# Top-k attention with a smooth-ReLU MLP: top-k over pairs of scores, and the mask by a rectifier and a subtraction

## The chip, the cores and the metric

The kernel runs on one core of a Trainium2 chip. A core has five engines with queues of their own: TensorE (PE; its weight loads are shown apart as PEld), VectorE (DVE), ScalarE (ACT), GpSimd (POOL) and SyncE (SP), which here issues the DMAs. Each engine works off its instructions in one fixed order, and semaphores make it wait for others. The metric is the device time of one execution in microseconds. The kernel before takes 2017.08 us (median of 3 runs, 2016.96 to 2017.25).

## The reference

Two blocks, one behind the other. In attention (8 batches, 8 heads, 576 rows, head size 64), each row keeps only its 32 largest scores:

```python
scores = scale * np.matmul(q, k.transpose(0, 1, 3, 2))
kth = np.partition(scores, -top_k, axis=-1)[..., -top_k:-top_k + 1]
mask = scores >= kth
scores = np.where(mask, scores, -1000000000.0)
scores = scores - np.max(scores, axis=-1, keepdims=True)
attn = np.exp(scores)
attn = attn / (np.sum(attn, axis=-1, keepdims=True) + 1e-09)
return np.matmul(attn, v).astype(np.float32)
```

Its output, 4608 rows of 512, goes through an MLP of width 2048: `h = x @ w_in`, then 0 where h <= -1, h where h >= 1, and (h + 1)² / 4 between, then `@ w_out`. The two weights come as float64, everything else as float32.

## The kernel before, in words

**Steps.** A batch's 576 rows are four tiles of 128 rows and a tail of 64. A step handles one pair of heads of one tile (for a tail, two pairs of heads in the 128 partitions); there are 144 steps, `m` counts them. Each step has five parts:

- `scores` (L194): PE multiplies queries by keys into PSUM banks (L206), ACT copies them with the scale to `s` in SBUF (L209), [128, 2, 576]: 128 rows, two heads, 576 scores.
- `top_k` (L211), all on DVE: MAX8 (L218) gives the eight largest of a row, MATCH_REPLACE8 (L221; the profile shows a short MATCH_VALUE_LOAD ahead of it) strikes them out. Four rounds of MAX8 and three of striking out, for each of two heads, give the 32 largest; the last of `tops` is the threshold.
- `weights` (L230): POOL makes the negated threshold `nkth` (L233) and `nb` (L235). For each head ACT applies the mask, a Prelu with a huge slope below the threshold (L228), then Exp with the row's sum (L239). DVE makes the reciprocal of the sum (`z` L241, `rz` L242), POOL scales the row by it (L244).
- `transpose_w` (L247): PE transposes the weights (L254, L257), ACT copies them from PSUM to `wT` and `wTt` (L255, L258).
- `values` (L261): PE multiplies by v into `po` (L269, L277), ACT copies the result to `xT` (L282, L284), the MLP's input.

**The MLP.** It runs over chunks of one or two row tiles. `hidden` (L297) makes 128 hidden units: PE into a bank `ph` (L300; three banks), ACT `r` (L304), POOL its square (L306), DVE the clamp `g` (L307). `final` (L310) multiplies by w_out into `py` (L315), ACT copies it to `y` (L319; two buffers), SP stores it.

**The weights.** `weight_piece` (L78) turns 512 float64 columns into float32, as SP loads them: DVE takes the bits apart (L85, L86, L90), ACT converts the low word (L92) and takes a magnitude (L97), POOL puts them together (L93, L94), DVE writes the result (L98). There are 32 such pieces. The tiles between have one buffer each, so a piece follows another.

**Order.** PE's order is the program's. Pass `m` of the main loop (L407) puts on it: `values` of step m-2, scores of m+1, MLP work, `transpose_w` of m-1, queries and keys to come, MLP work. `top_k` and `weights` of step m come in the same pass. `advance` (L365) hands out the MLP's work, by costs, evenly over the steps left, but only as far as the pieces are converted; `convert` (L357) converts `PER_STEP` (L53) pieces a step. The order on the other engines is made when the program is built, from the dependences and estimated costs. The tiles of scores, transposes and values share a ring of four PSUM banks (tag `a`): PE can't go on until ACT has emptied one.

**Loads.** SP issues all DMAs in one queue: values and keys of the next batch, queries two tiles ahead (tails in `q_tl`, L136, two buffers), weight pieces, and the stores of `y`.

Of the kernel before, what the change touches and what calls it, by code (L numbers as in the profile page):

```python
# [11 lines left out]
U32 = mybir.dt.uint32  # L12
AF = mybir.ActivationFunctionType
# [3 lines left out]
TOP_K = 32  # L17
# [4 lines left out]
def kernel(  # L22
# [30 lines left out]
    PER_STEP = 3  # L53

    const = ctx.enter_context(tc.tile_pool(name="const", bufs=1))
    xtp = ctx.enter_context(tc.tile_pool(name="xtp", bufs=3))
    stage = ctx.enter_context(tc.tile_pool(name="stage", bufs=2))
    att = ctx.enter_context(tc.tile_pool(name="att", bufs=2))
    ps = ctx.enter_context(tc.tile_pool(name="ps", bufs=1, space=PSUM))

# [15 lines left out]
    WC = 512  # L76
# [37 lines left out]
    def whole(x, b):  # L114

        return x[b, :, 0:SM, :].rearrange("h (p c) d -> p h c d", c=NT)

    def load_values(b):
        v_in = stage.tile([P, H, NT, D], F32, name="v_in")
        nc.sync.dma_start(out=v_in, in_=whole(v, b))  # L120
        v_tl = v_tails[b % 2]
        for j in range(2):
            nc.sync.dma_start(out=v_tl[0][j * TL:(j + 1) * TL, j::2, :],
                              in_=v[b, j::2, SM:S, :].rearrange("h p d -> p h d"))
        for hp in range(NHP):
            g = hp % 2
            nc.sync.dma_start(out=v_tl[1][g * TL:(g + 1) * TL, 2 * hp:2 * hp + 2, :],
                              in_=v[b, 2 * hp:2 * hp + 2, SM:S, :].rearrange("h p d -> p h d"))
        return v_in, v_tl

    def load_queries(b, t):
        if t < NT:
            q_in = stage.tile([P, H, D], F32, name="q_in", bufs=2)
            nc.sync.dma_start(out=q_in, in_=whole(q, b)[:, :, t, :])
        else:
            q_in = stage.tile([TL, H, D], F32, name="q_tl", bufs=2)  # L136
            nc.sync.dma_start(out=q_in, in_=q[b, :, SM:S, :].rearrange("h p d -> p h d"))
        return q_in


    def main(i):
        return slice(0, SM) if i == 0 else slice(TL, S)

    def tail(i):
        return slice(SM, S) if i == 0 else slice(0, TL)

    def pieces(i, j, c0, c1):

        if i == j:
            return [(c0, c1, c0)]  # L150
        cuts = [(0, TL, SM), (TL, S, 0)] if i else [(0, SM, TL), (SM, S, 0)]
        return [(max(a, c0), min(b, c1), o + max(a, c0) - a) for a, b, o in cuts if max(a, c0) < min(b, c1)]


    def keys_of(b):

        kT = stage.tile([P, NHP, S], F32, name="kT")
        v_in, v_tl = load_values(b)
        k_tl = stage.tile([TL, H, D], F32, name="k_tl", bufs=1)
        nc.sync.dma_start(out=k_tl, in_=k[b, :, SM:S, :].rearrange("h p d -> p h d"))  # L160
        for hp in range(NHP):
            k_in = stage.tile([P, NT, 2, D], F32, name="k_in")
            for j in range(2):
                nc.sync.dma_start(out=k_in[:, :, j, :], in_=whole(k, b)[:, 2 * hp + j])
            pt = ps.tile([P, NT, P], F32, name="pk", tag="a", bufs=4)
            for c in range(NT):
                nc.tensor.transpose(pt[:, c, :], k_in[:, c].rearrange("p j d -> p (j d)"), ident)
            for j in range(2):
                d = slice(j * D, (j + 1) * D)
                nc.scalar.copy(kT[d, hp, main(j)], pt[d].rearrange("p c n -> p (c n)"))  # L170
            if hp == 0:
                pt = ps.tile([P, NHP, TL], F32, name="pkt", tag="a", bufs=4)
                for h2 in range(NHP):
                    nc.tensor.transpose(pt[:, h2, :], k_tl[:, 2 * h2:2 * h2 + 2].rearrange("p j d -> p (j d)"),
                                        ident[0:TL, 0:TL])
                for j in range(2):
                    d = slice(j * D, (j + 1) * D)
                    nc.scalar.copy(kT[d, :, tail(j)], pt[d])
            yield dict(kT=kT, v=v_in, v_tl=v_tl)

    def queries_of(q_in, t):
        n = P if t < NT else TL
        qT = stage.tile([P, NHP, n], F32, name="qT" if t < NT else "qTt")
        pt = ps.tile([P, NHP, n], F32, name="pq", tag="a", bufs=4)
        for hp in range(NHP):
            nc.tensor.transpose(pt[:, hp, :], q_in[:, 2 * hp:2 * hp + 2].rearrange("p j d -> p (j d)"),
                                ident[0:n, 0:n])
        nc.scalar.copy(qT, pt)
        return qT
# [4 lines left out]
    def scores(st):  # L194
        t, hp, kT, qT = st["t"], st["hp"], st["keys"]["kT"], st["qT"]
        st["s"] = s = att.tile([P, 2, S], F32, name="s", bufs=3)
        for hf in range(2):
            sp = [ps.tile([P, SH], F32, name="sp", tag="a", bufs=4) for _ in range(2)]
            c0, c1 = hf * SH, (hf + 1) * SH
            for i in range(2):  # L200
                for j in ([i] if t < NT else [0, 1]):
                    d = slice(j * D, (j + 1) * D)
                    g = hp if t < NT else hp + i
                    o = sp[i] if t < NT else sp[i][j * TL:(j + 1) * TL]
                    for a0, a1, k0 in pieces(i, j, c0, c1):
                        nc.tensor.matmul(o[:, a0 - c0:a1 - c0], qT[d, g, :], kT[d, g, k0:k0 + a1 - a0],  # L206
                                         start=True, stop=True)
            for i in range(2):
                nc.scalar.activation(s[:, i, c0:c1], sp[i], AF.Copy, scale=SCALE)  # L209

    def top_k(st):  # L211
        s = st["s"]
        rest = att.tile([P, 2, S], F32, name="rest", bufs=1)
        st["tops"] = tops = att.tile([P, 2, TOP_K], F32, name="tops", bufs=3)
        src = s
        for r in range(0, TOP_K, 8):
            for i in range(2):
                nc.vector.max(out=tops[:, i, r:r + 8], in_=src[:, i, :])  # L218
            if r + 8 < TOP_K:
                for i in range(2):  # L220
                    nc.vector.match_replace(out=rest[:, i, :], in_to_replace=tops[:, i, r:r + 8],  # L221
                                            in_values=src[:, i, :], imm_value=LOWEST)
                src = rest
# [3 lines left out]
    def mask(x, nkth):  # L227
        nc.scalar.activation(x, x, AF.Prelu, bias=nkth, alpha=FAR)  # L228

    def weights(st):  # L230
        s, tops = st["s"], st["tops"]
        nkth = att.tile([P, 2], F32, name="nkth")
        nc.gpsimd.tensor_scalar(nkth, tops[:, :, TOP_K - 1], -1.0, 1.0, ALU.mult, ALU.mult)  # L233
# [151 lines left out]
    for got in keys_of(0):  # L385
        keys[0] = got
# [78 lines left out]
```

## Time and profile before

| | |
|---|---|
| median of 3 runs | 2017.08 us |
| the profiled execution | 2018.67 us |
| its span, first to last instruction | 2016.9 us |
| mean granted TensorE clock | 0.927 |
| first 33 us: loads, first keys | PE busy 11.6, DVE 10.9 us |
| MAX8 at 128x576 (1152 of them) | 748 to 750 ns each |
| MATCH_REPLACE8 at 128x576 (864) | 743 ns each |
| mask and Exp on ACT, 128x576 | 772 and 770 ns each |
| scaling on POOL, 128x576 | 768 ns each |
| two-input operation on POOL, 128x256 and 128x512 | 612 and 1271 ns each |

The profile gives for each engine the busy time, in slices and by groups of instructions with one line, and for each wait the instruction that ended it. A mean duration of one instruction is longer than the distance between the starts of two, since one begins before the other has ended. "PE sp L206 <- ACT xT L282: 54.3, 33, 5.1" means that the matmuls of line 206 waited 54.3 us in all, 33 times and 5.1 us at the longest, and that ACT's instruction of line 282 ended the wait. A granted clock of 1.0 is TensorE's full speed.

### The profile page before, as it was taken

What the parts mean: (1) busy time and instruction counts of PE and PEld (TensorE: products, weight loads), DVE (VectorE), ACT (ScalarE), POOL (GpSimd) and SP (SyncE); (2) the same over time, 40 slices, a digit from 0 to 9 for tenths busy, and PEclk for the clock granted to TensorE, in tenths of its full rate; (3) what the DMA queues carried; (4) which work ended last, traced back from release to release, by engine and by line L of the source; (5) the groups of instructions that cost most, each with busy time, mean ns of one, the idle gap of its engine ahead of it and who ended that gap; (6) DMA issues with size and microseconds to landing.
All of it is one profiled execution on the core that took longest, in us unless ns stands there. A gap on an engine that the chain in (4) does not pass through costs nothing.

```text
span 2016.9 us, 29329 instructions
## 1 busy us (share of the span) xinstructions
PE 1717.6 (85%) x10128; PEld 1175.6 (58%) x10128; DVE 1608.3 (80%) x3648; ACT 1075.0 (53%) x2589; POOL 537.6 (27%) x1003
## 2 busy tenths in 40 slices
PE   3245488989989999989898999888999999998999
PEld 2243266557566666656565666656474765765666
DVE  4878789989897887889786887888787787968861
ACT  4545546565555654565555555565454555545442
POOL 2564522213221221213121222213131231321321
PEclk7667798999999999989998999999999999999999
DMA  6232200100011001100011000110010000000000
GB/s 162 78 92 75 68 14 18 41 22 12 21 30 30 22 3 29 33 22 11 21 30 29 22 1 23 28 35 11 14 33 21 17 6 11 6 16 6 1 11 11
DMA packets 102803, 57.45 MB, mean 28 GB/s; under 512 B 85760, under 2 KB 93952, under 8 KB 102656
## 3 DMA queue, kind: packets, MB, share of 16 engines
q1 hardware_dynamic: 102656, 55.59, 10.0%
q8 instruction: 80, 1.31, 0.3%
q14 instruction: 67, 0.55, 0.1%
HBM read 46.14 MB, written 9.44 MB: 28 GB/s over the span
## 4 chain that ended last, share of the span: by engine, by line
DVE 53%; PE 19%; ACT 12%; POOL 10%; issue 6%; DMA 1%; SPq 0%; POOLq 0%; DVEq 0%; ACTq 0%
DVE tops L218 27%; DVE rest L221 20%; PE py L315 9%; PE ph L300 4%; ACT s L228 4%; ACT s L239 3%; DVE g L307 3%; POOL s L244 3%; ACT s L209 2%; POOL r L306 2%; PE sp L206 2%; POOL low L93 2%; PE po L269 2%; POOL low L94 2%; PE pw L254 2%
## 5 line engine op out<-in xcount | busy, mean ns | idle before, releaser
L300 PE MATMUL ph<-xT,w_in 128*128 128x256 f32 (+1 forms) x2816 | 560.4, 355 | 72.0 <-DVE g L307 71.8
L218 DVE MAX8 tops<-rest 128x8 f32<-128x576 f32 x864 | 619.5, 748 | 0.1
L315 PE MATMUL py<-w_out,g 128*128 128x512 f32 x1152 | 558.6, 630 | 45.1 <-DVE w_out L98 39.5
L300 PEld LDWEIGHTS ph<-xT,w_in 128*128 128x128 f32 x2816 | 466.2, 197 | 158.0 <-DVE g L307 87.9
L221 DVE MATCH_REPLACE8 rest<-tops,rest 128x576 f32<-128x576 f32 x576 | 424.1, 743 | 0.0
L315 PEld LDWEIGHTS py<-w_out,g 128*128 128x128 f32 x1152 | 217.5, 199 | 306.1 <-issue 238.0
L228 ACT ACTIVATE s<-s,nkth 128x576 f32<-128x576 f32 x288 | 214.4, 772 | 315.4 <-POOL nkth L233 315.2
L218 DVE MAX8 tops<-s 128x8 f32<-128x576 f32 x288 | 205.9, 750 | 202.7 <-ACT s L209 202.7
L244 POOL TENSOR_SCALAR s<-s,rz 128x576 f32<-128x576 f32 x288 | 217.6, 768 | 382.0 <-DVE rz L242 243.1
L306 POOL TENSOR_TENSOR r<-r 128x256 f32<-128x256 f32 (+1 forms) x352 | 187.8, 540 | 423.6 <-ACT r L304 418.4
L206 PE MATMUL sp<-kT,qT 64*128 64x288 f32 x1024 | 196.8, 452 | 60.2 <-ACT xT L282 51.2
L304 ACT ACTIVATE r<-ph,half 128x256 f32<-128x256 f32 (+1 forms) x352 | 148.2, 433 | 172.8 <-PE ph L300 141.3
L255 ACT COPY wT<-pw 128x512 f32<-128x512 f32 x288 | 155.9, 587 | 132.8 <-PE pw L254 131.7
L239 ACT ACTIVATE s<-s,nb 128x576 f32<-128x576 f32 x288 | 221.6, 770 | 1.2
L254 PE MATMUL pw<-ident,s 128*128 128x128 f32 x1152 | 163.5, 288 | 68.8 <-POOL s L244 64.1
L209 ACT ACTIVATE s<-sp 128x288 f32<-128x288 f32 x576 | 198.7, 410 | 36.3 <-PE sp L206 34.7
L221 DVE MATCH_REPLACE8 rest<-tops,s 128x576 f32<-128x576 f32 x288 | 212.6, 743 | 0.0
L254 PEld LDWEIGHTS pw<-ident,s 128*128 128x128 f32 x1152 | 142.9, 149 | 119.5 <-POOL s L244 72.6
L307 DVE SCALAR_TENSOR_TENSOR g<-ph,r 128x256 f32<-128x256 f32 (+1 forms) x352 | 128.6, 368 | 76.4 <-POOL r L306 71.3
L233 POOL TENSOR_SCALAR nkth<-tops 128x2 f32<-128x2 f32 x144 | 29.1, 202 | 571.1 <-DVE tops L218 571.1
L206 PEld LDWEIGHTS sp<-kT,qT 64*128 64x128 f32 x1024 | 108.4, 194 | 108.0 <-ACT xT L282 66.0
L269 PEld LDWEIGHTS po<-wT,v_in 128*64 128x64 f32 x2048 | 120.1, 143 | 85.6 <-issue 41.3
(51 smaller groups left out, 1086.7 us busy)
## 6 DMA issues: line engine op xcount, KB each, us to landing
q_in<-in_q_dram SPq DMA_DIRECT2D x32, 256.0 KB, 3.1
v_in<-in_v_dram SPq DMA_DIRECT2D x8, 1024.0 KB, 5.9
k_in<-in_k_dram SPq DMA_DIRECT2D x64, 128.0 KB, 3.2
raw<-in_moe_w_in_dram SPq DMA_DIRECT2D x16, 512.0 KB, 3.9
raw<-in_moe_w_out_dram SPq DMA_DIRECT2D x16, 512.0 KB, 3.5
out_dram<-y SPq DMA_DIRECT2D x32, 256.0 KB, 2.3
v_tail<-in_v_dram SPq DMA_DIRECT2D x16, 64.0 KB, 2.5
k_tl<-in_k_dram SPq DMA_DIRECT2D x8, 128.0 KB, 3.2
```

What stands on the lines that cost most here:

```text
L206: nc.tensor.matmul(o[:, a0 - c0:a1 - c0], qT[d, g, :], kT[d, g, k0:k0 + a1 - a0], start=True, stop=True)
L209: nc.scalar.activation(s[:, i, c0:c1], sp[i], AF.Copy, scale=SCALE)
L218: nc.vector.max(out=tops[:, i, r:r + 8], in_=src[:, i, :])
L221: nc.vector.match_replace(out=rest[:, i, :], in_to_replace=tops[:, i, r:r + 8], in_values=src[:, i, :], imm_value=LOWEST)
L228: nc.scalar.activation(x, x, AF.Prelu, bias=nkth, alpha=FAR)
L239: nc.scalar.activation(s[:, i, :], s[:, i, :], AF.Exp, bias=nb[:, i:i + 1], accum_out=z[:, i:i + 1])
L244: nc.gpsimd.tensor_scalar(s[:, i, :], s[:, i, :], rz[:, i:i + 1], 1.0, ALU.mult, ALU.mult)
L254: nc.tensor.transpose(pt[:, c, :], w[:, i, main(i)][:, c * P:(c + 1) * P], ident)
L300: nc.tensor.matmul(ph, w_in[:, kk, f * P:(f + 1) * P], xT[:, kk, 0:cw], start=(kk == 0), stop=(kk == NK - 1))
L306: nc.gpsimd.tensor_tensor(out=r, in0=r, in1=r, op=ALU.mult)
L307: nc.vector.scalar_tensor_tensor(out=g[:, 0:cw], in0=ph, scalar=1.0, in1=r, op0=ALU.max, op1=ALU.min)
L315: nc.tensor.matmul(py, gs[f][:, i * P:(i + 1) * P], w_out[:, f, :], start=(f == 0), stop=(f == NF - 1))
```

## The change

- **Top-k by pairs.** Score c is paired with score c + 288. DVE writes the larger of each pair to `more` and the smaller to `less`, [128, 2, 288] each. The four rounds run on `more`, in place; one MAX8 on `less` gives its eight largest, `seconds`. The 32nd of all is the largest among the 32nd of `more` and eight minima of the 31st down to the 24th of `more` with the first to the eighth of `seconds`: one small minimum and one MAX8 over nine elements per head.
- **The general path.** This is right unless more than seven smaller scores belong to the top 32. POOL writes, for each row, the eighth of `seconds` less the threshold to `excess`. After all steps, the largest of `excess` becomes a flag, which every engine reads; if it is above zero, the whole computation runs again with the top-k of before (`run(inner, False)`). This second copy of the program lies behind a branch.
- **The mask.** ACT writes Relu of 2⁸⁰ times (threshold - score) to `far`, and POOL subtracts that from the scores. Both heads' masks come ahead of both heads' Exps; the bias of Exp is the negated maximum.
- **Smaller tiles.** Weight pieces have 256 columns instead of 512, 64 instead of 32, with `PER_STEP` 6 instead of 3. `q_tl` has one buffer instead of two.

Everything from the pools to the main loop is put into `run(ctx, paired)`; lines that are only indented by this are left out.

```diff
-    PER_STEP = 3
+    PER_STEP = 6
...
+    n_steps = B * (NT * NHP + NHP // 2)
+    excess = const.tile([P, 2 * n_steps], F32, name="excess")
-    WC = 512
+    WC = 256
...
+    def run(ctx, paired):
...
-            q_in = stage.tile([TL, H, D], F32, name="q_tl", bufs=2)
+                q_in = stage.tile([TL, H, D], F32, name="q_tl", bufs=1)
...
+        def rounds_of(tops, src, rest, n):
+            for r in range(0, n, 8):
+                for i in range(2):
+                    nc.vector.max(out=tops[:, i, r:r + 8], in_=src[:, i, :])
+                if r + 8 < n:
+                    for i in range(2):
+                        nc.vector.match_replace(out=rest[:, i, :], in_to_replace=tops[:, i, r:r + 8],
+                                                in_values=src[:, i, :], imm_value=LOWEST)
+                    src = rest
+        def top_k(st):
+            s = st["s"]
+            tops = att.tile([P, 2, TOP_K + 8], F32, name="tops", bufs=3)
+            if paired:
+                more = att.tile([P, 2, SH], F32, name="more", bufs=1)
+                less = att.tile([P, 2, SH], F32, name="less", bufs=1)
+                nc.vector.tensor_tensor(out=more, in0=s[:, :, 0:SH], in1=s[:, :, SH:S], op=ALU.max)
+                nc.vector.tensor_tensor(out=less, in0=s[:, :, 0:SH], in1=s[:, :, SH:S], op=ALU.min)
+                seconds = att.tile([P, 2, 8], F32, name="seconds")
+                kth = att.tile([P, 2, 8], F32, name="kth", bufs=3)
+                rounds_of(tops, more, more, TOP_K)
+                rounds_of(seconds, less, None, 8)
+                nc.vector.tensor_tensor(out=tops[:, :, TOP_K:TOP_K + 8], in0=tops[:, :, TOP_K - 2:TOP_K - 10:-1],
+                                        in1=seconds, op=ALU.min)
+                for i in range(2):
+                    nc.vector.max(out=kth[:, i, :], in_=tops[:, i, TOP_K - 1:TOP_K + 8])
+                st["kth"] = kth[:, :, 0]
+                m = st["m"]
+                nc.gpsimd.tensor_tensor(out=excess[:, 2 * m:2 * m + 2], in0=seconds[:, :, 7], in1=kth[:, :, 0],
+                                        op=ALU.subtract)
+            else:
+                rounds_of(tops, s, att.tile([P, 2, S], F32, name="rest", bufs=1), TOP_K)
+                st["kth"] = tops[:, :, TOP_K - 1]
+            st["max"] = tops[:, :, 0]
...
     def weights(st):
-        nkth = att.tile([P, 2], F32, name="nkth")
-        nc.gpsimd.tensor_scalar(nkth, tops[:, :, TOP_K - 1], -1.0, 1.0, ALU.mult, ALU.mult)
-        nb = att.tile([P, 2], F32, name="nb")
-        nc.gpsimd.tensor_tensor(out=nb, in0=tops[:, :, TOP_K - 1], in1=tops[:, :, 0], op=ALU.subtract)
+            nmax = att.tile([P, 2], F32, name="nmax")
+            nc.gpsimd.tensor_scalar(nmax, st["max"], -1.0, 1.0, ALU.mult, ALU.mult)
+            bound = att.tile([P, 2], F32, name="bound")
+            nc.gpsimd.tensor_scalar(bound, st["kth"], FAR, 1.0, ALU.mult, ALU.mult)
+            far = att.tile([P, 2, S], F32, name="far", bufs=1)
         z = att.tile([P, 2], F32, name="z")
         for i in range(2):
-            mask(s[:, i, :], nkth[:, i:i + 1])
-            nc.scalar.activation(s[:, i, :], s[:, i, :], AF.Exp, bias=nb[:, i:i + 1], accum_out=z[:, i:i + 1])
+                nc.scalar.activation(far[:, i, :], s[:, i, :], AF.Relu, bias=bound[:, i:i + 1], scale=-FAR)
+                nc.gpsimd.tensor_tensor(out=s[:, i, :], in0=s[:, i, :], in1=far[:, i, :], op=ALU.subtract)
+            for i in range(2):
+                nc.scalar.activation(s[:, i, :], s[:, i, :], AF.Exp, bias=nmax[:, i:i + 1], accum_out=z[:, i:i + 1])
...
+    with ExitStack() as inner:
+        run(inner, True)
+    flag = const.tile([1, 8], I32, name="flag")
+    with tc.tile_pool(name="end", bufs=1) as end, tc.tile_pool(name="endps", bufs=1, space=PSUM) as endps:
+        worst = end.tile([P, 8], F32, name="worst")
+        nc.vector.max(out=worst, in_=excess)
+        pt = endps.tile([1, P], F32, name="pt")
+        nc.tensor.transpose(pt, worst[:, 0:1], ident)
+        top = end.tile([1, 8], F32, name="top8")
+        nc.vector.max(out=top, in_=pt)
+        nc.vector.tensor_scalar(flag, top, 0.0, None, ALU.is_gt)
+    again = nc.values_load(flag[0:1, 0:1], min_val=0, max_val=1)
+    with tc.If(again > 0):
+        with ExitStack() as inner:
+            run(inner, False)
```

## The prediction, as it was put on record

> **What bounds the kernel now.** First the page's shares and slices.
>
> ```profile
> PE 1717.6 (85%) x10128; PEld 1175.6 (58%) x10128; DVE 1608.3 (80%) x3648; ACT 1075.0 (53%) x2589; POOL 537.6 (27%) x1003
> PE   3245488989989999989898999888999999998999
> DVE  4878789989897887889786887888787787968861
> PEclk7667798999999999989998999999999999999999
> ```
>
> PE is nearly full from the sixth slice on, DVE at eight or nine tenths. Before that PE is a third busy: two regimes. The busy times by stretch (x is the count) give them numbers.
>
> ```profile
> 33.00:270.00 237.00, 110.83 (x633) 79.79 (x634) 190.05 (x406) 116.24 (x253) 118.99 (x134) 0.69 0.25 75
> 270.00:1960.00 1690.00, 1542.22 (x9141) 1051.78 (x9140) 1394.67 (x3184) 930.03 (x2271) 403.27 (x831) 0.96 0.07 19
> 1960.00:2016.90 56.90, 52.94 (x310) 35.68 (x309) 12.70 (x38) 16.16 (x41) 10.18 (x25) 0.99 0.03 10
> ```
>
> The columns are PE, its weight loads, DVE, ACT, POOL, granted clock. Of the 144 steps (one pair of heads of one row tile each; counted by the nkth instructions), 12 begin before 270 us, 131 in the middle, one after. In the middle a step takes 1690/131 = 12.9 us: PE 11.8 busy, DVE 10.6, POOL 3.1. PE waits 1690 - 1542 = 148 us in all; that is the stock the change can draw on there. The waits of the middle stretch (total, times, longest) say for whom:
>
> ```profile
> PE sp L206 <- ACT xT L282: 54.3, 33, 5.1
> PE ph L300 <- DVE g L307: 37.1, 28, 4.3
> PE pw L254 <- POOL s L244: 13.9, 5, 6.3
> PE po L269 <- ACT wT L255: 10.2, 9, 3.3
> ACT s L228 <- POOL nkth L233: 287.9, 113, 7.3
> DVE tops L218 <- ACT s L209: 200.5, 78, 7.4
> DVE z L241 <- ACT s L239: 44.1, 15, 5.1
> ```
>
> PE waits mostly for PSUM banks that ACT hasn't emptied: with the smaller lines for xT, wT and wTt (8.3, 7.9, 3.8, 2.4) 87 us. ACT in turn stands 288 us at the mask (L228), which needs the 32nd score, so DVE. But DVE itself stands 200 us for scores. The chain of waits gives 53% to DVE, 19% to PE. So PE is the floor, and DVE's passes make part of what is above it.
>
> At the start the timeline shows another bound, the conversion of the weights:
>
> ```profile
> 55.09 0.62 DVE L241 TENSOR_SCALAR z<-z 128x2 f32<-128x2 f32 x1
> 57.01 2.16 POOL L244 TENSOR_SCALAR s<-s,rz 128x576 f32<-128x576 f32 x2
> 63.61 0.69 DVE L98 SCALAR_TENSOR_TENSOR w_in<-size,low 128x512 f32<-128x512 f32 x1 [1.34 <-POOL low L94]
> ```
>
> Steps take 20.0 us there (nkth at 51.78, 71.79, 91.81); one weight piece follows another through DVE, POOL (1.27 + 1.26 us) and DVE again, and DVE idles 1.34 us in most of them.
>
> **DVE, step by step.** Four MAX8 in a row take 2.64 us (chain, at 1011.43), 0.66 each; two replacements with their loads 1.46, 0.73 each. Now: 8 x 0.66 + 6 x 0.73 = 9.66 us a step. No row shows a 288-wide pass. Slope from L307: 416 ns at 256 elements, 283 at 128, 1.04 ns per element, so 288 fewer save 0.30 us: 0.36 and 0.43. After: 10 MAX8 (8 on the larger, 2 on the smaller) 3.6; 6 replacements 2.6; two pairing operations, nearest L98 with two SBUF inputs, started 0.61 apart at 512, so 0.68 at 576: 1.36; three tiny ones at z's and rz's 0.15 to 0.19: 0.5. Sum 8.06, **1.6 us a step less**. Ends: nothing saved by width, 10 x 0.66 + 6 x 0.73 + 1.86 = 12.8 (3.2 more); all halved, 7.4 (2.3 less). I take 8.06, since both L307 widths stand in one run.
>
> **The path from threshold to weights.** nkth and nb become nmax and bound, 0.2 us each as before; ACT keeps four passes of 0.77. New are two subtractions on POOL. Its two-input rows are 612 ns at 256 and 1,267 at 512, 2.56 ns per element: 1.43 us at 576, 2.86 a step, and 0.2 for excess. POOL goes from 3.1 to 6.2 us a step. Mask to last Exp took 3.2 us (1012.85 to 1016.05); now 0.4 + 0.77 + 2.86 + 0.95 = 5.0 and handoffs, **2.0 us longer**. Transposes of a step are issued some 8 us after its scaling ended (1019.2 to 1027.2), which hides the 2.0; without that cover it is 2.0 x 131 = 262 us.
>
> POOL and DVE hinder each other: the scale pair took 2.16 us beside L98 and L85, elsewhere 1.47. The Trainium skill (GPSIMD Engine Reference, Specifications) says why: they share SBUF interfaces, and a DVE instruction with two SBUF inputs, or in a two-port mode, contends. That speaks against this change, whose pairing operations have two SBUF inputs and run while POOL subtracts; by it term (b) below would be at its upper end, +87 instead of +39.
>
> **Terms, against the profiled execution (span 2016.9, 2018.67 with what lies around it).**
> - (a) PE's waits for ACT's banks and for s: 87 + 14 = 101 us. DVE earlier by 1.6 us a step frees the mask sooner. Two thirds, **-67** (ends 0 and -101): ACT's order stays a queue, so not all.
> - (b) Hidden units (L300). A 256-wide one takes 1.9 us; three banks let PE run two ahead, 3.8 us, and a bank returns after r, square, g: 0.47 + 0.61 + 0.42 + some 0.3 = 1.8. Slack 2.0. Two subtractions queued ahead of the square make 2.86, 0.9 over it; with the pairing's 1.36 in the way 2.2 over. Hidden units fill 514 of 1,690 us, 30%. 131 x 0.30 x 1.0 = **+39** (ends 0 and, at 2.2, +87). The scale pair (1.47) stayed inside the slack so far. Behind a late g stand the next step's passes on DVE.
> - (c) Clock. At 0.96, PE's 1,542 us hold some 62 that full speed would save; transposes that follow a wait take 2.0 us, others 1.04. In proportion to the waits, -67 + 39 = -28 of 148: **-12** (ends -42 and +37, by a and b's ends).
> - (d) Start, 12 steps. A piece's serial part is 0.61 + 0.33 + 0.59 + 0.33 + 0.22 + 2.65 = 4.7 us, 14.2 for three. Six half pieces: DVE's 1.86 becomes 1.06 (256 elements fewer at L307's slope, half of that for L85 and L90, which start 0.33 apart at 512), handoff 0.22, POOL 1.33 (612 ns twice and gaps): 2.6, 15.6 together, so 1.4 more. Subtractions of 2.86 come into the same POOL queue, DVE gives 1.6: between -1.6 (all that is new is hidden) and +4.3 a step (no gain of DVE felt); I take +1: **+12** (ends -20 and +52). ACT's pieces and the 32 more loads on SP (0.33 each to issue) are hidden behind this.
> - (e) The last 57 us are PE alone: hidden units and output products, unchanged. Behind them the flag: two MAX8, a transpose, a compare, a register load on each engine, the branch. Arithmetic from rows: 0.75 + 0.29 + 0.2 + 0.2 = 1.4; the register load at the nearest, a DMA's landing, 2.3, with the last y's DMA (2.3) beside it. **+5** (ends 0 and +15). The Trainium skill (Advanced Engine Details and Errata, Control Flow Timing) gives about 108 ns for a compare-and-branch; by it (e) would be about +2; no row here shows one.
> - (f) q_tl with one buffer: the last pair's two tails are loaded next to each other, so the second load waits for the first's transposes, up to four steps; queued behind it on SP are y's stores, one per some 48 us with two y buffers, which hide it. Without that cover one store late, 0 to 48 us. I take 0.
>
> Sum: -67 + 39 - 12 + 12 + 5 = -23, so 2018.67 - 23 = 1995.7; the median stands 1.6 under the profiled execution: **1994 us**.
>
> **Rivals.**
> - *PE's floor reached.* For: DVE has 200 us of waiting already, and falls to 9.0 us a step against PE's 11.8. Against: POOL's doubled load. (a) -101, (b) 0, (c) -42, (d) -20, (e) +2: 1856 us; the case reaches up to 1955.
> - *Slower: DVE stands at z.* DVE runs in a fixed order; z (L241) lies between the next step's rounds, 3.4 us behind the last MAX8 (1012.7 to 1016.1). The second Exp now ends 2.0 us later. If z keeps its place, DVE stands up to 2.0 us a step with the next rounds queued behind it, and the mask behind those. It decides once this wait eats the 1.6 us freed: (a) 0, (b) +39, (c) +16, (d) +12, (e) +5: 2089. At 2.0, with 0.4 x 131 = 52 on PE and (c) +38: 2163. For: L98's 1.34 us of idling shows an order that puts DVE too early behind POOL. Against: z waited in only 15 of 131 steps.
> - *Hidden anyway.* PE's 92% leaves no net: (a) and (b) cancel, 2013 to 2021.
> - *The change doesn't do what it says:* the general path runs too. It would need a row with eight pairs that lie wholly in its top 32. Worked out from the reference's inputs, the most is six (the largest excess is -0.0009), so the branch is not entered. If it were: some 4,000 us.
>
> **Chances.** Forecast (1955 to 2013) 0.41, floor 0.13, z 0.38, hidden 0.07, branch 0.01. Faster by over 0.2% (about what a measurement of this kernel can tell from no change) 0.54, within 0.07, slower 0.39. The likeliest case's own range is 1955 to 2013. The range reaches into the floor (0.05 of it lies below 1905) and into z's case (0.13 above 2090), with the branch 0.19 left out: 1905 to 2090.
>
> **What would show it.** MAX8 at 0.36 and replacement at 0.43 us between starts (not: the DVE step). L233's wait on ACT falls below 288 us and PE's waits for xT below 54 (not: a). PE's wait for g rises from 37 toward 76 (b). POOL's subtractions last 1.4 us, longer beside the pairing. DVE's wait at z stays near 44 us; over 200 is the slower rival. First steps near 21 us (d). The span behind the last output product grows by 5 us (e).

## The result, and the profile after

The changed kernel takes 2239.19 us (median of 4 runs, 2235.35 to 2242.14), the kernel before 2017.02 on the same chip: 1.111 times as long, 95% interval 1.108 to 1.114. The forecast was 1994 with a range up to 2090. The profiled execution took 2235.35 us, its span is 2233.4, 216.5 longer than before.

Shares and slices of the changed kernel:

```profile
PE 1793.4 (80%) x10129; PEld 1212.1 (54%) x10129; DVE 1450.4 (65%) x4787; ACT 1098.8 (49%) x2653; POOL 1015.6 (45%) x1499
PE   3443477888888898898988898887989888898898
DVE  5786666767676666667676665666576666756651
PEclk7665689889999999999999999988989999999999
```

DVE's busy time fell from 1608 to 1450 us. PE does the same work in 1793 us instead of 1718, and its share of the span fell from 85% to 80%.

Busy times by stretch; the cuts are where POOL makes `bound` from the threshold of the first, the 13th and the last step:

```profile
33.92:320.08 286.16, 128.65 (x698) 90.12 (x699) 201.31 (x622) 128.01 (x322) 166.83 (x237) 0.66 0.21 64
320.08:2178.85 1858.77, 1607.00 (x9121) 1083.63 (x9120) 1231.38 (x4107) 944.13 (x2268) 831.63 (x1226) 0.93 0.07 17
2178.85:2233.40 54.55, 46.13 (x265) 30.18 (x263) 5.82 (x21) 13.40 (x33) 10.82 (x22) 0.96 0.04 12
```

Cut at the same place (`nkth`), the kernel before has 242.2, 1692.1 and 49.1 us. So the start lost 44 us, the 131 steps of the middle 167 (1.27 a step), the end 5. In the middle PE's busy time rose from 1544 to 1607 as its clock fell from 0.96 to 0.93; its idle time rose from 148 to 252. The waits of that stretch (total, times, longest):

```profile
ACT far L267 <- POOL bound L263: 312.8, 120, 6.4
DVE more L238 <- ACT s L216: 237.7, 108, 6.4
DVE z L272 <- ACT s L270: 216.9, 54, 8.1
PE sp L213 <- ACT xT L313: 124.8, 62, 7.3
ACT s L270 <- POOL s L268: 106.3, 183, 1.0
PE ph L331 <- DVE g L338: 39.6, 30, 4.6
PE po L300 <- ACT wT L286: 25.3, 14, 7.1
PE pw L285 <- POOL s L275: 17.0, 3, 7.9
```

What should have fallen rose: PE's wait for xT from 54 to 125 us, ACT's at the mask from 288 to 313. DVE's wait at z rose from 44 to 217. New is ACT's wait at Exp (L270) for the subtraction. In the timeline of ACT it looks like this:

```profile
1776.40 1.44 ACT L267 ACTIVATE far<-s,bound 128x576 f32<-128x576 f32 x2 [5.20 <-POOL bound L263]
1778.69 0.78 ACT L270 ACTIVATE s<-s,nmax 128x576 f32<-128x576 f32 x1 [0.85 <-POOL s L268]
...
1780.05 0.77 ACT L270 ACTIVATE s<-s,nmax 128x576 f32<-128x576 f32 x1 [0.49 <-POOL s L268]
...
1780.82 0.24 ACT L313 COPY xT<-po 128x128 f32<-128x128 f32 x1
1780.97 1.35 ACT L216 ACTIVATE s<-sp 128x288 f32<-128x288 f32 x4
```

ACT stands 0.85 and 0.49 us. Behind the two Exps in its queue lie the copy of xT, whose bank PE needs for the next scores, and the four score copies, which DVE needs for the next top-k. The matmuls that this copy reads had ended at 1776.86, some 4 us before it starts. In the same stretch PE and DVE stand:

```profile
1781.12 0.75 PE L213 MATMUL sp<-kT,qT 64*128 64x288 f32 x2 [3.09 <-ACT xT L313]
1780.95 0.17 DVE L272 TENSOR_SCALAR z<-z 128x2 f32<-128x2 f32 x1 [5.02 <-ACT s L270]
```

Not every step looks like this: where the values come late, the copy of xT waits for PE and not for ACT. But the chain of work that ended last takes this way in many steps, from the mask over the subtraction and Exp to the score copies and the next step's pairing. Here is one:

```profile
982.85 0.78 ACT far L267
983.71 1.41 POOL s L268
985.14 0.87 ACT s L270 x2
986.01 0.90 ACT s L216 x3
986.94 0.76 DVE more L238
```

At the start, half pieces follow one another like this:

```profile
185.39 0.43 DVE L98 SCALAR_TENSOR_TENSOR w_out<-size,low 128x256 f32<-128x256 f32 x1 [1.71 <-POOL low L94]
187.75 0.72 POOL L94 TENSOR_TENSOR low<-low,top 128x256 f32<-128x256 f32 x1
188.51 0.43 DVE L98 SCALAR_TENSOR_TENSOR w_out<-size,low 128x256 f32<-128x256 f32 x1 [1.70 <-POOL low L94]
```

That is 3.12 us from one half piece to the next, with nothing else in the way.

### The profile page after: what moved, and what is told of

Its sections match the earlier page's. It is cut to its first block, busy times and chain, and to the rows that moved or that the text cites. A ratio compares the mean times of both kernels' runs of the same rounds, so it can differ in the third digit from the quotient of the medians.

```text
span 2233.4 us, 31360 instructions
## 1 busy us (share of the span) xinstructions
PE 1793.4 (80%) x10129; PEld 1212.1 (54%) x10129; DVE 1450.4 (65%) x4787; ACT 1098.8 (49%) x2653; POOL 1015.6 (45%) x1499
## 4 chain that ended last, share of the span: by engine, by line
PE 27%; POOL 22%; issue 21%; DVE 15%; ACT 14%; DMA 1%; POOLq 0%; SPq 0%; ACTq 0%; DVEq 0%
PE ph L331 12%; POOL s L268 9%; PE py L346 7%; ACT far L267 5%; POOL s L275 4%; ACT s L216 3%; ACT s L270 3%; DVE more L238 3%; DVE tops L222 3%; POOL r L337 3%; PE sp L213 3%; DVE less L239 2%; POOL low L93 2%; POOL low L94 2%; DVE more L225 2%
## 5 line engine op out<-in xcount | busy, mean ns | idle before, releaser
L222 DVE MAX8 tops<-more 128x8 f32<-128x288 f32 x1152 | 476.7, 446 | 0.0
L268 POOL TENSOR_TENSOR s<-s,far 128x576 f32<-128x576 f32 x288 | 407.2, 1429 | 120.2 <-ACT far L267 116.6
L225 DVE MATCH_REPLACE8 more<-tops,more 128x288 f32<-128x288 f32 x864 | 376.3, 441 | 0.0
L267 ACT ACTIVATE far<-s,bound 128x576 f32<-128x576 f32 x288 | 212.4, 770 | 327.2 <-POOL bound L263 327.2
L213 PE MATMUL sp<-kT,qT 64*128 64x288 f32 x1024 | 229.7, 462 | 135.7 <-ACT xT L313 112.4
L275 POOL TENSOR_SCALAR s<-s,rz 128x576 f32<-128x576 f32 x288 | 242.7, 853 | 157.9 <-DVE rz L273 119.5
L238 DVE TENSOR_TENSOR more<-s 128x576 f32<-128x576 f32 x144 | 138.8, 964 | 242.3 <-ACT s L216 242.3
L270 ACT ACTIVATE s<-s,nmax 128x576 f32<-128x576 f32 x288 | 223.6, 777 | 118.8 <-POOL s L268 117.5
L250 POOL TENSOR_TENSOR excess<-seconds,kth 128x2 f32<-128x2 f32 x144 | 32.6, 226 | 478.7 <-DVE kth L247 452.6
L300 PE MATMUL po<-wT,v_in 128*64 128x128 f32 x2048 | 161.0, 293 | 28.9 <-ACT wT L286 28.4
```

The source lines that it names most:

```text
L267: nc.scalar.activation(far[:, i, :], s[:, i, :], AF.Relu, bias=bound[:, i:i + 1], scale=-FAR)
L268: nc.gpsimd.tensor_tensor(out=s[:, i, :], in0=s[:, i, :], in1=far[:, i, :], op=ALU.subtract)
L270: nc.scalar.activation(s[:, i, :], s[:, i, :], AF.Exp, bias=nmax[:, i:i + 1], accum_out=z[:, i:i + 1])
L275: nc.gpsimd.tensor_scalar(s[:, i, :], s[:, i, :], rz[:, i:i + 1], 1.0, ALU.mult, ALU.mult)
```

## The experiments

Where two edits are compared, the parts are taken from marks in the traces: the time at which POOL makes `nkth` or `bound` of the 13th step, and the mean step from there to the last.

| kernel | us | 13th step at | mean step |
|---|---|---|---|
| before | 2017 | 275.7 | 12.92 |
| changed | 2239 | 320.1 | 14.19 |
| before, half pieces (e4) | 2054 | 308.8 | 12.93 |
| pairing, old mask, half pieces (e2) | 2059 | 296.5 | 13.05 |
| new mask, old top-k, half pieces (e3) | 2185 | 330.6 | 13.76 |
| pairing alone, whole pieces (e12) | 2016 | 257.1 | 13.02 |
| shorter top-k (e11) | 1965 | 259.9 | 12.62 |
| pairing, order turned (e14) | 1869 | 256.4 | 11.89 |
| before, order turned (e15) | 1909 | 274.6 | 12.07 |
| changed, Exps behind (e9) | 2160 | 320.4 | 13.65 |
| changed, Relus behind (e16) | 2103 | 322.2 | 13.19 |
| changed, both behind (e17) | 2016 | 328.8 | 12.49 |

### Which part costs what

**e1.** One copy of the program, without flag and branch.

```diff
...
-    again = nc.values_load(flag[0:1, 0:1], min_val=0, max_val=1)
-    with tc.If(again > 0):
-        with ExitStack() as inner:
-            run(inner, False)
```

> The changed kernel without its flag, its branch and the second copy of the program; nothing else differs, so it is the base of the next two. Theory 1 (the mask: two subtractions on GpSimd lengthen the way from threshold to weights, and VectorE and ScalarE stand in their fixed order): 2232 to 2236 us, only the end gets shorter by some 5 us (the last stretch behind the last mask is 5.4 us longer after the change than before). Theory 2 (the pairing on VectorE is the cost): the same. Theory 3 (the general path behind the branch costs, by fetching of instructions or by the order made for the other engines): 2150 us or less.

2239.43 us (2238.21 to 2240.09). The general path costs nothing that can be measured. The runs below that change this kernel (e2, e3, e8 to e10, e12 to e14, e16 to e18) also have one copy.

**e2.** One copy, with the old mask.

```diff
-                nc.scalar.activation(far[:, i, :], s[:, i, :], AF.Relu, bias=bound[:, i:i + 1], scale=-FAR)
-                nc.gpsimd.tensor_tensor(out=s[:, i, :], in0=s[:, i, :], in1=far[:, i, :], op=ALU.subtract)
...
+                nc.scalar.activation(s[:, i, :], s[:, i, :], AF.Prelu, bias=nkth[:, i:i + 1], alpha=FAR)
```

> The one-copy kernel with the mask of before: Prelu in place and Exp, head by head, no subtraction on GpSimd; top-k by pairs stays, weight pieces of 256 columns stay. Theory 1: VectorE's 222 us at z fall to about 50, the wait of ScalarE for the subtraction (117 us) is gone, and the time falls to 1960 to 2040 us (before, less what 1.6 us a step on VectorE bring, plus up to 40 us of the first steps for the half pieces). Theory 2: over 2150 us.

2058.91 us (2057.54 to 2060.73), between the two theories: most of the loss is gone, but DVE's wait at z fell only to 158 us in the middle, not to 50.

**e3.** One copy, new mask, old top-k.

```diff
-        run(inner, True)
+        run(inner, False)
```

> The other half: top-k of before over all 576 scores, with the new mask (rectifier, subtraction on GpSimd), pieces of 256 columns, one copy. Theory 1: the mask alone costs, 2180 to 2350 us (VectorE has 1.6 us a step less room than in the changed kernel). Theory 2: 2020 to 2080 us, near before.

2184.99 us (2183.97 to 2186.18). ACT waits 98 us at Exp in the middle.

**e4.** The kernel before with half pieces.

```diff
-    PER_STEP = 3
+    PER_STEP = 6
...
-    WC = 512
+    WC = 256
...
```

> The kernel before with weight pieces of 256 columns, 6 a step, instead of 512 and 3. Theory 1 and 2: the first 12 steps get longer by 10 to 40 us, nothing later: 2027 to 2057 us. If the 44 us that the first 12 steps lost come from the half pieces alone: 2055 to 2065 us. If from the subtractions in GpSimd's queue alone: 2012 to 2022 us.

2054.09 us (2053.16 to 2054.45). Against the kernel before in the same runs (2018.5) half pieces cost 36 us, 33 of them in the first 12 steps. On top of that the pairing alone costs 5 (e2), the new mask alone 131 (e3), and both 185 (e1): a surplus of 49. These prices hold what came along in e1, e2 and e3: one buffer of `q_tl` instead of two, in e1 and e2 the subtraction for `excess`, in e1 and e3 both masks ahead of both Exps.

### Suspects that fell

**e5.** The kernel before with two rounds of top-k instead of four.

```diff
-        for r in range(0, TOP_K, 8):
+        for r in (0, TOP_K - 8):
```

> The kernel before (512 columns, Prelu) with two of its four rounds of MAX8 and one of three of striking out per head... in numbers, it does rounds 1 and 4 only, so that it leaves out 4 MAX8 and 4 replacements a step; the weights are then those of the wrong threshold. VectorE has 4 x 0.66 + 4 x 0.73 = 5.6 us less a step, 800 us less in all. It asks what room on VectorE is worth at all. Theory A (VectorE's passes were no bound in the long middle stretch; PE's own order and what it waits for from ScalarE is): 1940 to 2015 us. Theory B (VectorE's chain is the bound, and the pairing gave too little): 1800 us or less.

1796.33 us (1795.51 to 1797.78). 776 us less of VectorE (1608 to 832 busy) gave 221 us, so DVE's passes do count: 0.28 us for each. By that the pairing, which takes 231 us off DVE (e12), should have given some 65.

**e6.** The kernel before with both masks ahead of both Exps, as the changed kernel has them.

```diff
             mask(s[:, i, :], nkth[:, i:i + 1])
+        for i in range(2):
             nc.scalar.activation(s[:, i, :], s[:, i, :], AF.Exp, bias=nb[:, i:i + 1], accum_out=z[:, i:i + 1])
```

> The kernel before with one thing moved: both heads' Prelu stand ahead of both heads' Exp, as in the new mask; no subtraction. If the order of the four passes on ScalarE is what the new mask costs: over 2080 us. If the subtraction on GpSimd is: 2010 to 2030 us.

2023.6 us (2016.1 to 2027.0), ratio 1.003 (1.001 to 1.004): the order of the passes isn't it.

**e7.** e4 with two more subtractions a step on POOL, 128x576 too, that nobody waits for.

```diff
...
+            junk = att.tile([P, S], F32, name="junk", bufs=2)
+            nc.gpsimd.tensor_tensor(out=junk, in0=idle_a, in1=nkth[:, i:i + 1].to_broadcast([P, S]), op=ALU.subtract)
```

> The kernel before with pieces of 256 columns (2054 us), and two more operations of 128x576 with two inputs on GpSimd in each step, where the subtractions would stand, but written to a tile that nobody reads: GpSimd has the load and shares its interface with VectorE, the way from threshold to weights has no new link. Theory 1a (the longer way, with ScalarE and VectorE standing for the subtraction, is the cost): 2055 to 2085 us. Theory 1b (GpSimd's load is the cost: squares for the MLP and scaling queue behind it, VectorE's two-input operations collide with it): 2130 to 2190 us, near the 2185 us of the new mask with the old top-k.

2057.13 us (2055.78 to 2058.43), 3 more than e4. One of these subtractions lasts 1151 ns, in e3 1416. At four fifths of the load, then, POOL's load alone costs next to nothing beside the old top-k; the subtraction costs because something waits for it.

**e8.** e1 with z, its reciprocal and the scaling emitted behind the next step's top-k.

```diff
...
+            if 1 <= m <= n:
+                scale(state[m - 1])
```

> The one-copy kernel (2239 us) with one thing moved: the sum's reciprocal (z, rz) and the scaling of a step come behind the top-k of the next step in the program, not ahead of it, so VectorE meets z some 7 us later. If VectorE's standing at z (222 us) is what the change costs: z's waits fall under 50 us and the time to 2080 to 2150 us. If it only hides waiting that comes from elsewhere (PE's order, GpSimd's queue): 2200 us or more, with the waiting moved to the scores or to PE's transposes.

2261.54 us (2257.3 to 2268.25). DVE still waits some 215 us at z, so the move didn't do what it was meant to, and 22 us are added. What this wait costs it doesn't say; what z waits for, the late Exp, is looked at next.

### ScalarE's queue

**e9.** e1 with the Exps of a step in the next pass, behind its score copies; z, its reciprocal and the scaling move along. The edge fixes only the order on ACT; it is no wait.

```diff
...
+            if 1 <= m <= n:
+                exps(state[m - 1], state[m + 1]["last"] if m + 1 < n else None)
...
+                if last is not None:
+                    tc.add_manual_dep(e.ins, last.ins.name, ORDER, reason="order")
```

> The changed kernel in one copy (no flag, no branch: 2239 us), with both Exp passes of a step moved to the next step and ordered behind its four score copies and the copy of xT. Nothing is left out or added. Theory A, ScalarE's standing at Exp for GpSimd's subtraction (106 us in the changed kernel) holds up the score and xT copies queued behind it, and PE with them: this standing goes to under 15 us, PE's waits for xT and for banks fall from 125 to under 80, and the time falls by 80 to 130 us, to 2110 to 2160. Theory B, what counts is how late the weights come, not what stands behind Exp: the Exps come later still, PE's waits for the scaled weights rise from 17 us to over 60, and the time stays at 2230 or goes above it. Theory C, the subtractions cost by their length on GpSimd alone: no change within 10 us of 2239.

2160.49 us (2160.13 to 2160.98), 79 less than e1. ACT's wait at Exp fell to 4 us. PE's waits in the middle:

```profile
PE pw L292 <- POOL s L282: 154.0, 86, 6.7
PE sp L214 <- ACT xT L320: 22.6, 25, 1.9
```

The wait for xT went from 125 to 23 us, as theory A has it; the weights now come late, 154 instead of 17, as theory B has it. A's gain is the larger, and 79 us are left of it.

**e10.** e1 with half of each subtraction.

```diff
-                nc.gpsimd.tensor_tensor(out=s[:, i, :], in0=s[:, i, :], in1=far[:, i, :], op=ALU.subtract)
+                nc.gpsimd.tensor_tensor(out=s[:, i, 0:SH], in0=s[:, i, 0:SH], in1=far[:, i, 0:SH], op=ALU.subtract)
```

> The changed kernel in one copy, with the subtraction done on 288 of the 576 columns only; the other half of the scores goes into Exp unmasked, so that part of the mask is left out. GpSimd's two operations fall from 1.43 to some 0.73 us each, 202 us of GpSimd in all, and so does the link between Relu and Exp. If the length of the link decides (theory A and B alike), about half or more of the 180 us between this kernel with the old mask (2059) and with the new one (2239) goes: 2130 to 2160. If the extra hand-overs between engines decide (ScalarE to GpSimd to ScalarE, of whatever length), most of it stays: 2200 to 2235. If GpSimd's load had nothing to do with it: 2239.

2117.09 us (2116.69 to 2119.61): 122 of the 180 us go with half the length, more than half. ACT's wait at Exp is 21 us in the middle. `more` and `less` also take 0.2 us a step less than in e1. The hand-overs alone aren't the cost.

**e11.** The kernel before without head 1's second round.

```diff
+                if (r, i) != (8, 1):
+                    nc.vector.max(out=tops[:, i, r:r + 8], in_=src[:, i, :])
...
+                    if (r, i) == (8, 1):
+                        continue
```

> The kernel before with one MAX8 and one replacement of a step left out (head 1's second round; its threshold is then a later score): 1.39 us a step, 200 us of VectorE, a little less than the pairing saves (231 us less busy). It prices the saving without the pairing's form. If the two-round kernel's slope holds from the first microsecond (221 us of time for 800 of VectorE, 0.28), it takes 1955 to 1970. If the first microseconds of VectorE are hidden and only a large saving comes through, it takes 2005 to 2020, and the pairing's saving could not have been worth more than that either.

1964.88 us (1964.82 to 1965.83), ratio 0.973 (0.971 to 0.975); head 1's threshold is its 24th score here. 54 us for 190 of VectorE (1608 to 1418 busy): the slope of e5.

**e12.** The pairing alone: e2 with whole pieces.

```diff
-    PER_STEP = 6
+    PER_STEP = 3
-    WC = 256
+    WC = 512
```

> The paired top-k alone on the kernel before: the old mask, whole weight pieces of 512, one copy. Half pieces cost 36 us and pairing 5 us where they were measured (2059 with both). If these add up, it takes 2017 to 2028: pairing alone is no gain. If the half pieces hid a gain of the pairing (conversion and pairing both in the first 12 steps), it takes under 2005, and beats both kernels.

2015.96 us (2013.69 to 2021.24), ratio 0.9987 (0.9973 to 1.0002). That can't be told from no change, though DVE does 231 us less. The start gains 19 us, the middle loses 13. What DVE saves in the middle (1397 to 1191 us busy), it stands: its wait for scores went from 200 to 226 us, at z from 44 to 157, for POOL's squares from 44 to 118.

Something changed in the order of ACT's instructions too. For the 131 steps after the first 12, counted by the starts in the traces, the first head's mask of a step lies ahead of all four score copies of the next step this often, and the second head's Exp too (the expectations of e14 and e16 have counts from the built programs, higher by one at most):

| program | mask ahead of all four | Exp ahead of all four |
|---|---|---|
| before | 61 | 7 |
| new mask, old top-k | 61 | 8 |
| pairing alone | 99 | 43 |
| changed | 98 | 43 |
| shorter top-k (e11) | 98 | 41 |

This order is made from dependences and estimated costs. Each shorter top-k has the mask further ahead, and where ACT then stands at the mask, the next scores lie behind it.

**e13.** e12 with the pairing's tail kept together.

```diff
...
+                for x in pair:
+                    if ends:
+                        behind(x, ends[-1])
...
```

> The paired top-k alone (old mask, whole pieces, one copy: 2016 us), with two orders fixed by hand and nothing left out: the next step's two pairing operations only behind this step's last MAX8 (they stand in front of it in some 14 of the 144 steps, 1.4 us each), and GpSimd's subtraction for the flag only behind nkth and nb (it stands ahead of them, 0.16 us in every step). If the pairing's lost gain lies in this tail, 20 + 23 us and some more in PE's waits come back: 1965 to 1985. If the tail isn't the cause: 2005 to 2020.

2014.28 us (2010.4 to 2015.35), ratio 0.998 (0.996 to 0.999). Not the tail.

**e14.** e12 with the mask ordered behind the next step's score copies. `behind(x, y)` puts x behind y on its engine, as the edge of e9 does; `last` is the last of a step's four score copies.

```diff
...
+                if st["m"] + 1 < n:
+                    behind(x, state[st["m"] + 1]["last"])
```

> The paired top-k alone (2016 us), with ScalarE's mask of a step ordered behind the four score copies of the next step; nothing is left out. In the order as built the mask stands ahead of all four in 100 of 131 steps (in the kernel before in 61): ScalarE stands at the mask for the threshold, the next scores wait behind it, and VectorE then stands for these scores (220 us, before 196). If this order eats the pairing's gain, VectorE's wait for scores falls below 100 us and the time to 1930 to 1985. If the mask's own lateness counts for more (weights later, PE's waits for them up from 14 us), it takes 2010 to 2070.

1868.72 us (1867.49 to 1870.75), ratio 0.926 (0.924 to 0.928). Waits in the middle of e12:

```profile
ACT s L266 <- POOL nkth L261: 302.5, 125, 6.0
PE sp L213 <- ACT xT L310: 75.7, 59, 4.6
ACT xT L310 <- PE po L297: 40.7, 33, 4.0
```

and of e14:

```profile
ACT xT L316 <- PE po L303: 261.3, 110, 7.4
ACT s L270 <- POOL nkth L265: 18.4, 16, 2.0
PE sp L217 <- ACT xT L316: 6.3, 3, 2.4
```

The waiting changed sides: PE waited for ACT's copy of xT, now ACT waits there for PE. ACT's standing at the mask is all but gone. The time fell below the expected 1930 to 1985, but not by the way that was expected: DVE's wait for scores rose from 226 to 280 us instead of falling below 100, while PE is nearly full now (1484 busy of 1557 us in the middle).

**e15.** The control: the same edge in the kernel before.

```diff
...
-            mask(s[:, i, :], nkth[:, i:i + 1])
+            x = mask(s[:, i, :], nkth[:, i:i + 1])
+            if st["m"] + 1 < n:
+                behind(x, state[st["m"] + 1]["last"])
```

> The control: the kernel before (2017 us) with the same order, mask behind the next step's four score copies. If the order is a cost of its own, which the kernel before pays in 61 of 131 steps too, it gains about 61/100 of what the paired kernel gains: 1970 to 2000. If the order only matters to the paired kernel: 2010 to 2025. If a later mask costs: over 2030.

1909.13 us (1906.77 to 1910.35), ratio 0.946 (0.944 to 0.947), a larger gain than any that was expected. The kernel before paid for its order too, 108 us. With the order turned the pairing is worth 1909 - 1869 = 40 us.

**e16.** The changed kernel (e1) with the Relus ordered behind the next score copies, by the same edge.

```diff
...
-                nc.scalar.activation(far[:, i, :], s[:, i, :], AF.Relu, bias=bound[:, i:i + 1], scale=-FAR)
+                x = nc.scalar.activation(far[:, i, :], s[:, i, :], AF.Relu, bias=bound[:, i:i + 1], scale=-FAR)
+                if st["m"] + 1 < n:
+                    behind(x, state[st["m"] + 1]["last"])
```

> The changed kernel in one copy (2239 us), with both Relus of a step ordered behind the next step's four score copies; nothing is left out. The Relu stands ahead of all four in 99 of 131 steps now. If the order of the queue makes the two edits dearer together than their sum (185 against 131 + 5), the surplus of 49 us and some of the mask's 131 come back: 2120 to 2195. If the mask's lateness counts for more: 2230 to 2300.

2103.16 us (2102.29 to 2107.94). 136 us come back, more than expected. ACT's wait at Exp is 218 us in the middle here.

**e17.** e16 with the Exps ordered behind the copy of wTt of the step before; z, its reciprocal and the scaling move along.

```diff
...
+            if m < n:
+                exps(state[m], state[m - 1]["copied"] if m >= 1 else None)
```

> The changed kernel in one copy with two orders on ScalarE: Relus behind the next step's four score copies (alone 2103 us), and Exps behind the copies of the step's transposed weights of the step before; nothing is left out. Theory A, ScalarE's standing at Exp (212 us at 2103) goes into the time: it falls below 70 us, and the time by 100 to 160 us, to 1945 to 2000. Theory B, the way from threshold to weights is what costs: the Exps come later still, PE's waits for scaled weights or for wT rise by the same amount, and the time stays at 2080 to 2140.

2016.31 us (2014.12 to 2019.52), ratio to the kernel before 0.999 (0.998 to 1.000). 87 us less than e16, near A's 100 and far from B. The two waits that the changed kernel had at 106 and 217 us:

```profile
DVE z L284 <- ACT s L280: 21.4, 19, 3.4
ACT s L280 <- POOL s L274: 17.6, 38, 0.9
```

Two orders on one queue are thus worth 223 us in the changed kernel, with the same instructions on every engine. That is as many as it had lost, but it doesn't make the order the whole cause: the kernel before gains 108 us by the first of them alone (e15). In that order the changed kernel is still 194 us behind it (2103 against 1909), and with both orders 107; the kernel before with the second as well wasn't run.

**e18.** e3 with the Relus behind the next score copies: e16 with the old top-k.

```diff
-        run(inner, True)
+        run(inner, False)
```

> Full-width top-k with the new mask in one copy and half pieces (2185 us without the order), Relus behind the next step's four score copies; nothing is left out. If the surplus of both edits together came from the order, the two edits add up here: the mask costs the same 198 us with either top-k, and this kernel takes 1945 + 198 = 2143, between 2125 and 2160. If the surplus has another cause (contention of the pairing with GpSimd, say), it takes 2075 to 2110, no more than the changed kernel in this order.

2102.89 us (2100.88 to 2103.73), as e16. Beside the new mask the pairing gives nothing even in this order, where it gives 40 beside the old one. So the surplus of both edits doesn't come from this order: here, too, it is some 40 us, for 49 in the order as built.

## Why the prediction was wrong

The step that failed is the path from threshold to weights. The prediction made it 2.0 us longer and set that at nothing, because the transposes come some 8 us later. It asked of the subtraction only how late the weights come, not what stands behind ACT while it waits: ACT works through one queue, in an order fixed beforehand. In terms of the sum, (a) had to fall by 67 us and rose by 94.

- **The way from threshold to weights.** From the threshold's first reading to the scaled weights it grew from 7.0 to 8.1 us (median), 1 us rather than 2, and PE's wait for weights stayed at 17 us (14 before): that cover held, as written. But between Relu and Exp ACT stands 0.8 us a step (106 us), and in many steps the copies that PE and DVE need wait with it. The new mask costs 131 us alone (e3 against e4); half the length of the subtraction brings 122 of the 180 us beside the pairing (e10), and e9 and e17 bring back 79 and 87 by letting ACT do copies meanwhile. What the rest of the mask's cost is isn't shown.
- **VectorE's arithmetic** was right for the passes: MAX8 446 ns for 748, replacement 441 for 743. With the old mask and whole pieces DVE saves 231 us, 1.6 a step (e12). In the changed kernel it saves 158: half pieces add 13 (e4), and the two pairing operations take 964 and 889 ns where 0.68 us was set for each.
- **(a)**, -67 for PE's waits for ACT's banks and for s: they went from 101 to 195 us. Two thirds was too simple a share. A faster DVE stood elsewhere for what it saved (e12), and the mask moved ahead of the next scores (61 to 98 of 131 steps). In the order as built the pairing costs 5 us with half pieces and gains 3 with whole ones, in the other it gains 40 (e14, e15). In neither is it 67.
- **(b)**, +39 for hidden units: PE's wait for g went from 37 to 40 us, but by two changes that nearly cancel. Beside the old top-k the new mask raised it by 39 us, from 39 (e4) to 78 (e3), just the forecast; the pairing with the old mask lowered it to 18 (e2), which the prediction hadn't foreseen. DVE's own wait for POOL's squares rose from 44 to 161 us in the changed kernel, and is 118 in e12 without the subtractions.
- **(c)**, -12 for the clock, up to +37: PE's busy time rose by 63 us for the same work, at a granted clock of 0.93 in the middle instead of 0.96. The sign followed the waits, as worked out, but those went the other way.
- **(d)**, +12 for the start, up to +52: +44. The half pieces alone cost 33 (e4). A half piece takes 3.12 us, not 2.6. The two POOL operations start 0.80 us apart and last 0.72 to 0.76, where the forecast used the 0.61 of another line's operation of that width; that is half of the difference, and DVE's operations with the hand-over to POOL are the other half. 0.52 us for each of 64 pieces is 33 us.
- **(e)**, +5 for flag and branch: the end is 5.4 us longer, and e1 finds no more. Right.
- **(f)** wasn't tried by itself.
- **The slower rival** named a sign that came (DVE's wait at z 44 to 217 us), but the sign doesn't tell the cause. Most of it is the shorter top-k: 157 us in e12, at the time of the kernel before. e8 didn't shorten the wait, and in e17 it went when the Exps, and z with them, were moved. What it costs by itself isn't shown.

Two things stay open. Pairing and e11 save about as much of VectorE (231 and 190 us) and have about the same order on ACT, but e11 gives 54 us and the pairing 3; the tail isn't it (e13). And both edits together cost some 40 to 50 us more than each for itself, in either order. In the turned order the rows fit one account that no run isolates: in e16 a subtraction takes 1594 ns beside the pairing, in e18 1417 beside the old top-k; 0.18 us on two of them in 144 steps makes 51 us on ACT's way to Exp. In the order as built that account fails, since a subtraction takes 1431 ns in e1 and 1416 in e3. There the pairing operations stretch instead, by 0.24 us a step against e2, which makes 35 us on DVE.

The paired kernel in the turned order (e14, 1869 us) beats both kernels.

## What to carry to other kernels

Before a pass is handed to another engine and back, read what lies behind it in the first engine's queue: here a stand of 106 us cost time because the next step's copies were behind it, and 79 us came back when they were put ahead. When a step on the way gets faster and the time doesn't follow, count how the built order changed: a wait that came to stand ahead of independent work can eat the gain. A single order edge tries this in one run; put it into the kernel before as well, which may gain from it too.

## What the runs showed of the hardware

POOL's tiny operations stretch beside DVE's operations with two inputs in SBUF. In e16, while `more` and `less` run on DVE (1018.01 to 1019.41):

```profile
1018.17 0.63 POOL L254 TENSOR_TENSOR excess<-seconds,kth 128x2 f32<-128x2 f32 x1 [3.44 <-DVE kth L251]
1018.77 0.69 POOL L267 TENSOR_SCALAR bound<-kth 128x2 f32<-128x2 f32 x1
```

Apart from such operations they take 0.20 and 0.19 us. The first ends as `more` does, the second as `less` does. It goes the other way too: `more` and `less` take 773 and 774 ns on the mean in e14, and 964 and 889 in the changed kernel. There `less` takes 0.75 us when POOL does nothing meanwhile, and 1.96 us in the 13 steps after the 12th in which it meets a subtraction. MAX8, with one input, takes 446 ns in the changed kernel with or without work on POOL beside it, and `g`, which has one of its two inputs in PSUM, doesn't stretch POOL's tiny operations. The Trainium skill (GPSIMD Engine Reference, Specifications) says that DVE and POOL share SBUF interfaces and that DVE instructions with two SBUF inputs contend; these rows agree.
